# Batch 0's attention in halves of the heads, its loads on two queues, and a re-timed plan

## The chip, the cores and the metric

The kernel runs on one core of one Trainium2 chip. A time is the device time of one execution in microseconds. The core's engines run side by side: PE (matrix products; its weight loads are listed as PEld), DVE and ACT (elementwise work), POOL (here only constants and the issue of DMAs) and SP (only the issue of DMAs). Each works through its instructions in the order in which the program holds them, and waits for the others through semaphores. All DMAs, whoever issues them, run on the core's 16 DMA engines.

## The reference

Eight batches of a linear attention with eight heads of 64, 576 tokens each, and behind it a feed-forward block over all 4608 tokens:

```python
theta = np.pi / 2.0 * pos / S
def phi(x, c, s):
    r = np.maximum(x, 0.0)
    return np.concatenate([r * c, r * s], axis=-1)
q_p, k_p = phi(q, cos_w, sin_w), phi(k, cos_w, sin_w)
kv = np.einsum('bhsf,bhsd->bhfd', k_p, v)
z = np.sum(k_p, axis=2)
num = np.einsum('bhsf,bhfd->bhsd', q_p, kv)
den = np.einsum('bhsf,bhf->bhs', q_p, z)[..., None] + 1e-06
x = (num / den).transpose(0, 2, 1, 3).reshape(B * S, H * D)   # 4608 x 512
h = x @ w_in                                                  # 512 x 2048
return (np.maximum(h, 0.0) ** 2) @ w_out                      # 2048 x 512
```

## The kernel before

A batch has 576 tokens: 512 "main" ones, held as 128 partitions of J = 4 columns (a token's place is 4p + j), and a tail of 64. The tail of heads 0 to 3 lies on partitions 0 to 63, that of heads 4 to 7 on 64 to 127; `HH` = 4 is half the heads.

Attention of a batch: load k, q (tile `kq`), v and their tails (`kqt`, `vst`); form the features (`cos_part`, `sin_part`: a relu times a column of cosines or sines, into `fe`; `cos_tail`, `sin_tail` into `fet`); copy v into `vext`, which has a column of ones for the sums z; sum k'v over the tokens on PE (`mm_kv`, into `kz`) and copy it out (`kvz`); transpose the query features (`tq`, copied to `qpT`); form numerators and denominators in one product (`mm_num`, into `num`); divide (`div`: add EPS into `den`, reciprocal, multiply into `xp`); and transpose x (`tx`, copied to `xT`). Batches 0 and 1 transpose on PE, later ones by DMA from SP's queue.

The feed-forward block: h = x w1 in units of 128 tokens x 2 by 256 columns (`hps`), then relu (`rt`) and square (`gT`), then the second product. Batch 0 and the first 16 units each of batches 1 and 2 are plain sums (`plan_plain1`); the others, and the second products of all batches but the first (`plan_pair`), use a seven-product scheme for 2 x 2 blocks, with sums of inputs made on DVE (`xs`, `w1s`, `w2t`, `gs`) and outputs combined from PSUM.

The opening, `begin`, is an order written out by hand. SP loads all of k. POOL issues the k tails, v, v's tails, then the constants (an iota; ACT makes the cosine and sine columns of it), the queries of columns 0 and 1 and of columns 2 and 3, four quarters of w1, the q tails, the first quarter of w2, and behind that batch 1's loads. PE multiplies zeros meanwhile (`warm`, 31 times, and some more further on). Then batch 0's first 256 tokens (columns 0 and 1) go through the whole attention, all eight heads at once: features of k, sums, features of q, transposes, numerators, division, x transposes. `xT` for these 256 tokens is complete when both columns' copies are done; the first units of the feed-forward block work on 128 tokens at a time, so that they can begin behind the first copy.

Everything behind the opening is ordered by a planner. Each step (`plan.op`) has its engine or engines, a modelled duration and what it follows; `plan.timeline` and `plan.dues` give due times back from the order of PE's products; `plan.run` goes through modelled time and lets each engine take the ready step with the smallest due time plus `SHIFT`. Steps that may run on ACT or DVE go where they would end first, unless `PINS` fixes them. What the opening leaves is told to the planner by `plan.given` with a time (when a w1 quarter has landed, when xT is there), and `plan.run` starts each engine at a given time. The planner's times decide the order of the instructions alone: on the chip an instruction runs when its inputs are there. The planner gives the product `mm_num` 0.49 us for a main column.

Of the kernel before, what the change touches and what calls it, by code (L numbers as in the profile page):

```python
# [24 lines left out]
    "qT0.3": -31.9, "xT0.4": 32, "H0.0.10.128": 13.4, "H0.0.11.0": 43.7, "H0.2.11.0": 11.5,  # L25
    "H0.3.11.0": 54.4, "cos1.2": -59.2, "sin1.2": -74.7, "cos1.3": -14, "qT1.0": 0.9,
    "num1.2": 43.7, "num1.3": 39.3, "xTc1.3": 132.4, "num1.4": 28.6, "Y0.5": -38.6, "Y0.6": -125,
    "w2t2": -56.9, "vs2.2": -129.7, "cos2.t": -52.5, "num2.4": 10.7, "H1.0.00.0": 55.6,
    "H1.0.01r": -26.6, "H1.1.00.0": 61.4, "H1.1.10.0": 30.6, "H1.1.01r": 32.5, "H1.2.10.0": 20.8,
    "H1.2.10q": -36.8, "H1.2.01q": -5.3, "H1.2.11.0": 68.3, "H1.3.00.0": 7.6, "ldv3.0": 13.8,  # L30
    "cos3.1": -16.4, "sin3.1": -8, "qTd3.1": -71.6, "qTd3.2": 11.2, "num3.4": 9,
    "H2.0.11.0": 10.4, "H2.2.10.0": 9.9, "H2.2.01.0": -74.6, "H2.3.00.0": 3.2, "H2.3.10.0": 44,
    "H2.3.10r": 24, "H2.3.11.0": -11.9, "Y1.P2": 25.1, "Y1.P5": -11.2, "Y1.P4": -63.2,
    "ldk4": -67.5, "cos4.0": 14.7, "cos4.2": 27.1, "sin4.3": 51.1, "xTd4.2": 62, "xs3.1": -57.3,
    "xs3.2": -36.1, "xs3.3": -21.9, "G3.1.P5": 7.9, "G3.1.P3": -74.8, "G3.1.c12q": -2.5,
    "G3.1.P4": 166.2, "G3.1.c21r": 6.2, "G3.2.P1": -10.4, "G3.2.P2": 13.6, "G3.2.c11r": 10.9,
    "G3.2.c12r": 3, "G3.2.c22q": 83.4, "G3.3.P5": 11.5, "G3.3.P2": 48, "Y2.P1": 45.5,
    "Y2.P6": 9.2, "Y2.P7": -8.1, "ldv5.0": -8.1, "sin5.1": -8.4, "cos5.2": -23.5, "sin5.2": -0.6,
    "sin5.3": -20.9, "num5.2": -9.7, "num5.3": -80.6, "G4.0.c21r": 93.6, "G4.1.c11q": 71,
    "G4.1.c12r": 1.5, "G4.1.c21q": 9.9, "G4.2.seed": -97.7, "G4.2.c11q": 9.2, "G4.2.P6": -0.3,  # L40
    "G4.2.P3": 7.6, "G4.2.c12r": 85.9, "G4.2.P4": 5.7, "G4.3.P5": 13.4, "G4.3.P6": 78.6,
    "Y3.S3": 42.1, "Y3.P6": -2.9, "Y3.P2": -11.9, "Y3.c12": 40.2, "ldq6": 30.5, "vs6.1": 87.7,
    "sin6.1": 32.5, "cos6.2": -22.7, "sin6.3": 55, "num6.0": 18.7, "div6.1": -32, "xTd6.0": 30.9,
    "num6.4": 28.3, "G5.0.c22r": 24.3, "G5.1.P3": 29.5, "G5.1.P7": -12, "G5.2.P7": 62.7,
    "G5.3.P7": -22.1, "G5.3.c22q": 8.8, "Y4.P2": -35.3, "Y4.P7": 59.5, "Y4.P5": 52.2,
    "Y4.c12": -21.2, "ldk7": -71.6, "ldkt7.1": -12.6, "num7.2": 38.6, "G6.0.P1": 17,
    "G6.0.P3": 44.1, "G6.0.P7": 30.6, "G6.2.P3": 69.8, "G6.2.c22q": 2, "G6.3.P1": -21.1,
    "G6.3.c12r": 53.8, "G6.3.c22r": -2, "Y5.P5": 68.2, "Y5.P3": 91.4, "G7.0.P4": 8.3,
    "G7.1.P7": 29.7, "G7.2.P7": 5.6, "G7.2.P4": 13.6, "G7.3.c12q": 16.8, "G7.3.c21q": 19.7,
    "Y6.P3": 22.2, "xs8.3": -26.6, "G8.1.P1": -33.6, "G8.2.P3": 16.2, "Y7.P7": 45.6,  # L50
    "Y7.P4": 15.3, "Y8.P20": 42.1, "Y8.P21": 43.7,
# [8 lines left out]
        "H0.1.01r H0.2.11q cos1.1 cos1.2 sin1.2 cos1.3 qTc1.1 xTc1.3 vs2.2 sin2.0 sin2.1 "  # L60
        "H1.3.01q cos4.0 cos4.1 cos4.2 sin4.3 sin4.t G3.2.c11q G3.2.c22q G3.2.c21q cos5.0 "
        "sin5.t G4.1.c12q G4.2.c11q G4.3.c11q G4.3.u2 G4.3.c22q Y3.s5 vs6.1 sin6.1 sin6.t "
        "G5.0.c21q G5.2.c11q G5.2.c22q vs7.0 vs7.2 G6.3.c22q"
    ),
    "DVE": (
        "H0.2.11r vs2.0 sin2.t H1.1.00r H1.2.01q H1.3.00r G3.1.c12q G3.1.c21r vs5.1 sin5.1 "
        "sin5.2 G4.0.c11q G4.1.c11q G4.1.c21q G4.2.c12q Y3.c21 vs6.2 G5.0.s5 G5.0.c22q "
        "G5.1.c11r G5.1.c21r G5.1.c21q G5.3.c22q G6.0.c11r G6.2.c22q G7.3.c12q G7.3.c21q "
        "G8.0.c11r Y8.s5"
# [290 lines left out]
def kernel(  # L360
# [215 lines left out]
    def load_main(nm, b, eng, j0=0, j1=J):  # L576
        eng.dma_start(
            out=kq[b][:, "kq".index(nm)][:, :, j0:j1], in_=main_of(nm, b)[:, :, j0:j1]
        )
# [22 lines left out]
    def fe_main(b, j, c0, c1, a=slice(0, 2)):  # L602
        return fe[b, j // 2][:, a, j % 2, :, c0:c1]

    def kq_main(b, j, a=slice(0, 2)):
        return kq[b][:, a, :, j, :]

    def cos_part(e, b, j, a=slice(0, 2)):
        feature(e, fe_main(b, j, 0, D, a), kq_main(b, j, a), cos_col[:, j : j + 1])

    def sin_part(e, b, j, a=slice(0, 2)):
        feature(e, fe_main(b, j, D, F, a), kq_main(b, j, a), sin_col[:, j : j + 1])

    def cos_tail(e, b, a=slice(0, 2)):
        feature(e, fet[b][:, a, :, 0:D], kqt[b][:, a], cos_col[:, J : J + 1])

    def sin_tail(e, b, a=slice(0, 2)):
        feature(e, fet[b][:, a, :, D:F], kqt[b][:, a], sin_col[:, J : J + 1])

    def mm_kv(b):  # L620
        for j in range(J + 1):
            for hh in range(HH):
                for half in range(2):
# [949 lines left out]
```

## Time and profile before

Three runs: 279.78, 281.14 and 284.09 us, median 281.14. The profiled execution took 279.59, of which its instructions span 277.4.

| what | from the profiled execution |
|---|---|
| busy share of the span | PE 97%, PE weight loads 82%, DVE 84%, ACT 66%, POOL 10% |
| granted PE clock | 0.999 on average |
| DMA | 53.00 MB, mean 191 GB/s |
| k of batch 0, 1 MB on SP, from issue to landing | 5.6 us |
| v of batch 0, 1 MB on POOL, from issue to landing | 7.6 us |
| last product on PE | starts 270.21, 1.91 us for the group of 16 |
| mean duration on DVE | 128x512 feature of batch 0 547 ns, its 128x256 tail 473, 128x1024 feature 760, square 420, relu from PSUM 688, `xp` 692, `vext` 128x1024 691 |
| mean duration on ACT | 128x512 feature 713 ns, 128x256 493, square 629, relu from PSUM 592, `qpT` 128x512 585 |

"PE" in the profile's lists is a product, "tile<-inputs" what it writes and reads; a group is several instructions of one kind in a row, and its length runs to the modelled end of the last, so that the next group can start before it.

### The profile page before, as it was taken

The numbers are of one execution on the slowest core, as the hardware profiler recorded it, in microseconds if no ns is written. First come the engines' busy times: TensorE is split into PE (matmuls) and PEld (weight loads), VectorE is DVE, ScalarE is ACT, GpSimd is POOL, SyncE is SP. The second block draws the span as 40 slices with busy tenths as digits, with TensorE's granted clock in tenths as the row PEclk, the third lists the DMA queues.
The fourth block names the chain that finished last, engine by engine and source line by source line (L and its number), as shares of the span: only waits on it lengthen the run. The fifth ranks groups of instructions, "written<-read, shape, count | busy, mean of one in ns | idle before, by whom it ended". The sixth has DMA issues, their size and how long they took to land.

```text
span 277.4 us, 6927 instructions
## 1 busy us (share of the span) xinstructions
PE 268.6 (97%) x2835; PEld 226.5 (82%) x2835; DVE 231.7 (84%) x453; ACT 184.3 (66%) x309; POOL 28.4 (10%) x46
## 2 busy tenths in 40 slices
PE   8999999999999999999999999999999999999992
PEld 2579856789889889888898888898888888888881
DVE  1779877898996979999999999999889959977921
ACT  3758863596967697699478967974457556756210
POOL 8835454100000000000000000000000000000000
PEclk9999999999999999999999999999999999999999
DMA  6999999989899999988876999751140001201014
GB/s 222 319 206 288 312 267 337 354 216 358 158 244 338 229 246 220 370 166 264 269 248 119 289 241 269 206 152 40 46 174 14 2 0 76 78 0 78 0 78 151
DMA packets 77503, 53.00 MB, mean 191 GB/s; under 512 B 52097, under 2 KB 72577, under 8 KB 77473
## 3 DMA queue, kind: packets, MB, share of 16 engines
q1 hardware_dynamic: 70128, 38.28, 51.6%
q0 software_dynamic: 7024, 13.76, 18.7%
q10 hardware_dynamic: 320, 0.52, 0.6%
q8 instruction: 22, 0.36, 0.6%
q14 instruction: 9, 0.07, 0.1%
HBM read 36.70 MB, written 9.44 MB: 166 GB/s over the span
## 4 chain that ended last, share of the span: by engine, by line
PE 74%; DMA 18%; DVE 3%; ACT 2%; issue 1%; POOL 0%; POOLq 0%; ACTq 0%; DVEq 0%
PE ya L537 17%; PE yb L537 15%; PE hb L537 11%; DMA kq<-in_q_dram 9%; PE hc L537 7%; PE ha L537 7%; PE hps L537 7%; DMA xT<-xp 4%; PE wm L537 4%; DMA vs<-in_v_dram 3%; PE kz L537 3%; PE num L537 2%; DMA qpTt<-fet 2%; PE yc L537 1%; ACT fe L524 1%
## 5 line engine op out<-in xcount | busy, mean ns | idle before, releaser
L537 PEld LDWEIGHTS <-w1sb 128*128 128x128 bf16 x800 | 73.8, 98 | 11.0 <-issue 2.7
L537 PEld LDWEIGHTS <-gs 128*128 128x128 bf16 x512 | 49.9, 98 | 6.0 <-DVE gs L534 0.2
L518 ACT ACTIVATE gT<-rt 128x512 bf16<-128x512 bf16 x77 | 47.5, 629 | 10.4 <-DVE rt L531 5.1
L537 PEld LDWEIGHTS <-gT 128*128 128x128 bf16 x448 | 43.5, 98 | 10.8
L537 PE MATMUL hps<-xT,w1sb 128*128 128x256 bf16 (+1 forms) x416 | 46.1, 264 | 1.1 <-ACT rt L512 0.4
L524 ACT ACTIVATE fe<-kq,cols 128x1024 bf16<-128x1024 f32 (+1 forms) x35 | 35.2, 1046 | 3.5 <-DMA kq<-in_q_dram 2.8
L537 PE MATMUL ya<-w2sb,gT 128*128 128x256 bf16 x256 | 30.6, 273 | 0.0
L537 PEld LDWEIGHTS <-w1s 128*128 128x128 bf16 x288 | 27.4, 98 | 3.6 <-issue 0.5
L520 DVE TENSOR_TENSOR gT<-rt 128x512 bf16<-128x512 bf16 x67 | 27.2, 420 | 3.7 <-ACT rt L512 3.0
L526 DVE TENSOR_SCALAR fe<-kq,cols 128x1024 bf16<-128x1024 f32 (+1 forms) x37 | 24.9, 714 | 5.5 <-DMA kq<-in_k_dram 5.1
L537 PE MATMUL hb<-xs,w1sb 128*128 128x256 bf16 x192 | 28.0, 273 | 0.0
L512 ACT ACTIVATE rt<-hps 128x512 bf16<-128x512 f32 x33 | 19.3, 592 | 7.5 <-PE hps L537 7.3
L537 PE MATMUL ha<-xT,w1sb 128*128 128x256 bf16 x160 | 24.0, 273 | 0.1
L663 DVE TENSOR_TENSOR xp<-num,den 128x512 bf16<-128x512 f32 (+1 forms) x33 | 22.3, 675 | 1.1
L534 DVE TENSOR_TENSOR gs<-gT 128x2048 bf16<-128x2048 bf16 x16 | 19.5, 1220 | 0.1
L531 DVE CUSTOM_DVE_ANT_0 rt<-hb,s 128x512 bf16<-128x512 f32 x24 | 16.3, 686 | 1.0 <-PE hb L537 0.7
L531 DVE CUSTOM_DVE_ANT_0 rt<-hc,u 128x512 bf16<-128x512 f32 x24 | 16.4, 685 | 0.2 <-PE hc L537 0.2
L508 ACT COPY hb<-ha 128x512 f32<-128x512 f32 x24 | 14.0, 581 | 4.0 <-DVE y L534 2.3
L508 ACT COPY u<-hb 128x512 f32<-128x512 f32 x22 | 12.8, 584 | 4.9 <-PE hb L537 4.9
L537 PE MATMUL yb<-w2sb,gs 128*128 128x256 bf16 x128 | 15.3, 273 | 0.0
L537 PE MATMUL yb<-w2t,gs 128*128 128x256 bf16 x128 | 15.3, 273 | 0.0
L537 PE MATMUL yb<-w2t,gT 128*128 128x256 bf16 x128 | 15.3, 273 | 0.0
(112 smaller groups left out, 401.1 us busy)
## 6 DMA issues: line engine op xcount, KB each, us to landing
out_dram<-y SPq DMA_DIRECT2D x16, 512.0 KB, 4.4
kq<-in_k_dram SPq DMA_DIRECT2D x6, 1024.0 KB, 6.2
kq<-in_q_dram SPq DMA_DIRECT2D x5, 1024.0 KB, 7.9
vs<-in_v_dram SPq DMA_DIRECT2D x10, 512.0 KB, 5.0
w1sb<-in_moe_w_in_dram POOLq DMA_DIRECT2D x4, 512.0 KB, 10.6
w2sb<-in_moe_w_out_dram POOLq DMA_DIRECT2D x4, 512.0 KB, 11.0
kq<-in_q_dram POOLq DMA_DIRECT2D x2, 1024.0 KB, 12.0
kq<-in_k_dram POOLq DMA_DIRECT2D x2, 1024.0 KB, 11.1
```

What stands on the lines that cost most here:

```text
L508: (nc.scalar.copy if e == "ACT" else nc.vector.tensor_copy)(out=out, in_=in_)
L512: nc.scalar.activation(out=out, in_=in_, func=ACTF.Relu)
L518: nc.scalar.activation(out=out, in_=in_, func=ACTF.Square)
L520: nc.vector.tensor_tensor(out=out, in0=in_, in1=in_, op=ALU.mult)
L524: nc.scalar.activation(out=out, in_=in_, func=ACTF.Relu, scale=col)
L526: nc.vector.tensor_scalar(out=out, in0=in_, scalar1=0.0, scalar2=col, op0=ALU.max, op1=ALU.mult)
L531: nc.vector._custom_dve(dve_ops.TENSOR_ADD_SAT, out=out, in0=in0, in1=in1, s0=BIG, s1=0.0)
L534: nc.vector.tensor_tensor(out=out, in0=in0, in1=in1, op=op)
L537: nc.tensor.matmul(out=out, lhsT=lhsT, rhs=rhs, start=start, stop=stop, skip_group_check=True)
L663: nc.vector.tensor_tensor(out=x.rearrange("p (b k) (l d) -> p b k l d", b=n, l=2), in0=n4[:, :, :, 0:D].rearrange("p b (k l) d -> p b k l ...
```

## The change

Three things.

Batch 0's opening works on two groups of four heads (A: heads 0 to 3, B: heads 4 to 7), one behind the other, with both columns of a group together. SP loads, for each group, k, the k tail and the v tail; POOL loads v and the queries of columns 0 and 1 for each group, with the constants between, then the first w1 quarter, the queries of columns 2 and 3, and the other w1 quarters. The order of the steps is written out anew, with 17 warming products at the start and others between the steps. The copies of `xT` go by kb (two of the four rows of x each), and the first two units of the feed-forward block are emitted in two parts each: kb 0 and 1, which need group A alone, and kb 2 and 3. All units now work on 256 tokens at a time; before, the first column's units of batch 0 worked on 128.

The planner's duration of a main numerator goes from 0.49 to 0.26, and the given times of the opening from 15.9 to 14.6 (first w1 quarter), 17.2 to 17.4 (features of columns 2 and 3), 13.3 to 12.6 (`kvz`), 16.4 and 17.4 to 14.2 and 15.6 (`xT`); the engines start at 14.6, 17.2 and 16.8 in place of 16.8, 17.4 and 17.1 (PE, ACT, DVE).

The tables `SHIFT` and `PINS` are replaced by others. The set of batches in plain sums (`PLAIN`) is the same in both.

```diff
 PINS = {
     "ACT": (
-        "H0.1.01r H0.2.11q cos1.1 cos1.2 sin1.2 cos1.3 qTc1.1 xTc1.3 vs2.2 sin2.0 sin2.1 "
...
+        "H0.0.01r sin2.t cos3.t H2.2.00q G3.2.s5 G3.3.c21q G4.0.c22q vs6.2"
...
             f"num{b}.{j}",
-            {"PE": 0.49 if j < J else 0.25},
+            {"PE": 0.26 if j < J else 0.25},
...
+        for part in range(parts):
+            kbs = range(part * KB // parts, (part + 1) * KB // parts)
...
         for g in range(2):
-            load_tail("k", 0, g, nc.gpsimd)
-        nc.gpsimd.dma_start(out=v0[:, :, :, :], in_=main_of("v", 0))
+            load_main("k", 0, nc.sync, heads[g])
+            load_tail("k", 0, g, nc.sync)
+            nc.sync.dma_start(out=vt0[rows_[g]], in_=tail_of("v", 0, g))
         for g in range(2):
-            nc.gpsimd.dma_start(out=vt0[g * TAIL : (g + 1) * TAIL], in_=tail_of("v", 0, g))
-        constants()
-        for i in range(2):
-            load_main("q", 0, nc.gpsimd, 2 * i, 2 * i + 2)
-        warm(31, "x0")
...
+            nc.gpsimd.dma_start(out=v0[:, heads[g]], in_=main_of("v", 0)[:, heads[g]])
+            load_main("q", 0, nc.gpsimd, heads[g], first)
+            if g == 0:
+                constants()
         for i in range(4):
             load_w1(i, 4)
+            if i == 0:
+                load_main("q", 0, nc.gpsimd, js=second)
...
+        def key_features(g, sin_tail_on):
+            for j in range(J):
+                cos_part("DVE", 0, j, k_, heads[g])
+                sin_part("ACT", 0, j, k_, heads[g])
+            cos_tail("DVE", 0, k_, rows_[g])
+            sin_tail(sin_tail_on, 0, k_, rows_[g])
+
+        def values(g):
+            dst = vx[:, :, heads[g], 0:D].rearrange("p j h d -> p h j d")
+            copy("DVE", dst, v0[:, heads[g]])
+            copy("DVE", vxt[rows_[g], :, 0:D], vt0[rows_[g]])
...
+        warm(17, "x0")
+        key_features(0, "ACT")
+        values(0)
+        za = kv_sums(0, "x1")
+        query_features(0)
+        kv_copy(0, za)
+        warm(1, "x0")
+        ta = turn_queries(0, "x2")
+        copy_queries("DVE", 0, ta, 0)
+        copy_queries("ACT", 0, ta, 1)
+        warm(3, "x0")
+        na = spare("n0", [P, 2, FP], F32, "num")
+        numerators(0, na)
+        key_features(1, "DVE")
+        div_den(na[:, :], dens[0])
+        values(1)
+        warm(6, "x0")
+        zb = kv_sums(1, "x3")
+        query_features(1)
+        div_mul(na[:, :], dens[0], x_of(0))
+        kv_copy(1, zb)
+        tb = turn_queries(1, "x4")
+        copy_queries("DVE", 1, tb, 0)
+        copy_queries("ACT", 1, tb, 1)
+        warm(3, "x0")
+        nb = spare("n0", [P, 2, FP], F32, "num")
+        numerators(1, nb)
+        xa = turn_x(0, "x5")
+        div_den(nb[:, :], dens[1])
+        div_mul(nb[:, :], dens[1], x_of(1))
+        for kb in range(2):
+            copy_x("ACT", 0, xa, kb)
+        warm(5, "x0")
+        xb = turn_x(1, "x1")
+        copy_x("DVE", 1, xb, 0)
+        copy_x("ACT", 1, xb, 1)
+        for j in (2, 3):
+            cos_part("DVE", 0, j, q_)
+            sin_part("ACT", 0, j, q_)
...
-        plan.timeline(rows, 16.8)
+        plan.timeline(rows, 14.5)
         plan.dues()
-        order = plan.run({"PE": 16.8, "ACT": 17.4, "DVE": 17.1, "POOL": 36.0, "SP": 46.0}, 44.2)
+        order = plan.run({"PE": 14.6, "ACT": 17.2, "DVE": 16.8, "POOL": 36.0, "SP": 46.0}, 44.2)
```

`numerators` writes a group's numerators of both columns into one tile, so that `div_den` and `div_mul` each treat the group's two columns in one instruction; `turn_queries`, `turn_x` and their copies do the transposes of one group.

## The prediction

> **What bounds the kernel now.** I read the page's busy times first, then the stages, then who PE waits for, then the opening in order of time, then the DMA issues. On the page:
>
> ```profile
> span 277.4 us, 6927 instructions
> ...
> PE 268.6 (97%) x2835; PEld 226.5 (82%) x2835; DVE 231.7 (84%) x453; ACT 184.3 (66%) x309; POOL 28.4 (10%) x46
> ```
>
> PE is the bound. The stages (stretch, its length, busy time by engine, granted clock, DMA share, GB/s) say where it is not:
>
> ```profile
> 0.00:4.00 4.00, 2.81 (x7) 1.01 (x8) 0.38 (x4) 1.28 (x1) 2.94 (x8) 1.00 0.41 116
> 4.00:8.00 4.00, 4.00 (x13) 1.43 (x12) 1.57 (x3) 1.99 (x5) 3.72 (x10) 1.00 1.05 375
> 12.00:17.00 5.00, 4.57 (x55) 2.78 (x56) 4.57 (x15) 4.12 (x7) 1.33 (x2) 1.00 1.24 215
> 22.00:272.00 250.00, 248.33 (x2647) 214.33 (x2645) 218.62 (x418) 172.07 (x289) 13.54 (x19) 1.00 0.69 186
> ```
>
> From 22 us to the last product PE idles 1.67 us in 250. The clock is 1.00 in every row. So the end moves only with the moment at which PE's real work begins, or with those 1.67 us. PE's waits after 18 us, largest first, are three of 0.3 to 0.4 us, of three kinds:
>
> ```profile
> PE hps L537 <- ACT rt L512: 0.4, 1, 0.4
> PE hc L537 <- DVE xs L534: 0.3, 1, 0.3
> PE hps L537 <- DMA xT<-xp: 0.3, 1, 0.3
> ```
>
> The opening in order of time (start, length, idle before in brackets): PE's 9.77 us of warming products are no work, and the first real product (hps) starts at 17.09.
>
> ```profile
> 1.19 9.77 PE L537 MATMUL wm<-zeros 128*128 128x512 bf16 x31 [1.19 <-DVE zeros L441]
> ...
> 11.81 1.33 ACT L524 ACTIVATE fe<-kq,cols 128x512 bf16<-128x512 f32 x2 [0.94 <-DMA kq<-in_q_dram]
> ...
> 17.09 0.61 PE L537 MATMUL hps<-xT,w1sb 128*128 128x128 bf16 x8
> ...
> 18.37 1.06 PE L675 MATMUL tq<-ident,fe 128*128 128x128 bf16 x16
> 19.27 1.06 PE L537 MATMUL hps<-xT,w1sb 128*128 128x128 bf16 x16
> 20.16 0.41 PE L537 MATMUL num<-kvz,qpT 128*128 128x65 bf16 x8
> ```
>
> DMA issues (KB, us from issue to landing), for issues of 7.9 to 10.4 us and then of 37 to 40 us:
>
> ```profile
> w1sb<-in_moe_w_in_dram POOLq DMA_DIRECT2D x3, 512.0 KB, 10.0
> ```
> ```profile
> kqt<-in_k_dram SPq DMA_DIRECT2D x2, 64.0 KB, 8.0
> kqt<-in_q_dram SPq DMA_DIRECT2D x2, 64.0 KB, 12.0
> ```
>
> The second quarter of w1 (issued at 8.81) thus lands at about 18.8; and 64 KB on SP takes 8 to 12 us while POOL's queue streams.
>
> **The opening, part by part.** Before, batch 0 needs k, v, both tails and the first two query columns, 2.75 MB, and the last of it releases the features at 11.81. From there it takes 6.1 us to the second copy of xT, which ends at 17.88 (17.29 + 0.59).
>
> After, the same 2.75 MB stand ahead of everything else, so I take group B's queries (heads 4 to 7) to land at the same 11.8 at the latest. The first 4 us move at 116 GB/s where the next 4 run at 375, because SP's k load has the engines to itself; POOL now issues v at 1.26 instead of 2.63. That can be worth between 0 and 0.9 us; I take 0.3: 11.5.
>
> From group B's queries to xT, everything is half as wide: sin on ACT twice (0.49 and 0.40, from the 128x256 row's 493 ns less the overlap of the 128x512 pairs) 0.9; hop and last transposes 0.5; ACT copy of qpT 128x512 0.59; hop, numerators, hop 0.5; den and reciprocal 0.17 + 0.20 + 0.07 of gaps; xp 128x512 0.69; x transposes with hops 0.5; copy 128x256 0.42 (the ACT row of xTt). The sum is 4.5: xT is complete at 16.0, against 17.88.
>
> This holds if DVE, which is in order, keeps up. Between group A's qpT copy and group B's xp it has, at its rows (128x256 features 0.27 to 0.41, bounded by the 128x256 cast and the 128x256 features of the tail; 128x1024 cast 0.69; 128x512 xp 0.69; half kvz 0.34 to 0.42; qpT 0.41; den pairs 0.37): eight features, two casts, two kvz/qpT copies, two xp and two den pairs, 5.5 to 6.7 us. Group A must then be through its qpT copy by 9.5 or so. A's inputs are 1.4 MB; before, 1.39 MB had moved by 6.4 us. So A's queries land between 6.4 (the two queues share evenly) and 9.3 (POOL's first transfer waits until SP's six loads are through, as it seems to before: the k tails that POOL issued at 1.26 took 5.0 us, landing just behind SP's k). I take 7.5; A's features, transposes and copy add 1.9: 9.4. That is just in time, and each us later moves xT by one.
>
> What comes next on PE is not xT alone. The built order is: two units (each in two parts by kb), 16 query transposes, one unit of the next column block, a numerator, then the rest. That third unit needs w1's second quarter. Its place in the byte order is unchanged (batch 0's loads, the first w1 quarter and the last query columns are all ahead of it, in either order), so it lands at 18.8, or up to 0.9 sooner. With xT at 16.0 the two units end at 17.0, the features of columns 2 and 3 (ACT, 1.33 behind the xT copy) at 17.3, the transposes at 18.2, and the third unit starts at 18.85, held by w1. Before, the same unit comes after the numerator's 0.25, at 20.41; without that, 20.16. The gain is 1.3 us. It stays 1.3 for any xT up to 16.5; from there on it shrinks one to one (third unit = xT + 2.3) and is nothing at 17.9. The parts are costed at nothing: w1's landing covers them; without that cover the first parts of both units, which can run before xT is complete, are worth up to 0.9.
>
> The 128-wide units become 256-wide: sixteen pairs take 0.89 (19.27 to 20.16), eight of the others 0.87 (a group of 16 at 0.109 each); four units give 0.1. Warming products fall from 39 to 35; they run only where PE waits anyway: nothing, and up to 0.9 if four of them (0.22 each) stood late in the chain. DVE's fet and vextt halves on 64 partitions add four instructions of 0.27 to 0.41, counted above.
>
> **The plan.** Of a numerator, the next product starts 0.25 behind it (20.16 to 20.41): the plan's 0.49 was 0.24 too much for some 30 of them, 7 us of plan time in which PE was really ahead. No instruction goes away. New shifts and pins move work between engines: in the built program DVE has 18 fewer relus and 13 more squares, six more wide features; at 0.69, 0.42 and 0.76 us that leaves DVE some 2 to 5 us lighter. Neither engine was the bound. Batch 2's first product, which waited 0.3 us for xT by DMA, now has three of batch 1's output products (1.75 us each) before it in place of two, so it does not need that transfer sooner. Loads for batches 1 and 2 keep their order on POOL except that k's second tail now stands behind the k and q loads; their DMA time is unchanged and PE has Y0's 14 us as cover. The idle 1.67 us can go to 0 or double; I take it as it is.
>
> **Sum.** 279.59 (profiled run: span 277.4 and 2.2 around it) less 1.3 gives 278.3. The three runs before are 279.78, 281.14, 284.09; the profiled one lies 1.5 under their median. I put the median after half a us above the sum: 278.8.
>
> **Rivals.**
>
> 1. *SP's second half starves.* SP's third to sixth loads (64 KB, 512 KB, 64, 64) run beside POOL's stream, and the rows above give 8 and 12 us to 64 KB there. Group B's v tail is issued at about 3.7 (0.46 and 0.65 each on SP), so it lands between 11.7 and 15.7. It decides from about 12.5 on, when DVE reaches that cast; DVE is in order, so everything behind waits. At 15.3, xT is complete at 20.0, the third unit starts at 22.3 instead of 20.16, and the kernel takes 281.7, slower than before. For it: the two rows. Against it: those SP tails were issued into a POOL queue already full, these at the very start. [...]
> 2. *POOL starts behind SP.* A's v lands at 8.6 and its queries at 9.3, DVE's chain ends at 18.2, third unit at 20.5: 279.9, no change. For it: the 5.0 us above.
> 3. *More.* The queues share from 3 us on and w1 lands 0.9 sooner, with 1.0 of the 1.67 us gone: 276.4.
> 4. *The tighter plan opens waits in the body*: 7 batches at one further wait of 0.4 (the largest now): 278.3 + 2.8 = 281.1.
> 5. *PE's clock falls in the longer waits of the opening.* The 31 warming products show the two rates: the weight loads come every 0.43 us up to 7.13, then 16 in 3.34. Seventeen end at about 7.8, and then PE waits for each group. If it fell back, some 6 us at half rate (1.19 to 7.13) cost 3: 281.3. [...]
>
> **Numbers.** Chances: forecast 0.47, rival 1 0.15, rival 2 0.13, rival 3 0.14, rival 4 0.07, rival 5 0.04. Range: 276.2 (rival 3) to 282.4 (rival 1, half a us over its sum); it leaves out combinations. 2% is 5.6 us, about what a measurement can tell from no change. Faster by that needs more than the opening's 1.3 to 2.2, all idle time and a lucky median: 0.06, from rival 3. Slower by that needs rivals 1 and 4 or 5 together: 0.07. Within: 0.87.
>
> **What would show it.** In the changed profile: the first hps at 14.5 to 15.5; the third unit's wait ended by the w1sb DMA, near 18.8; the first numerator behind it 1.3 us earlier than now; PE idle after 22 us near 1.7. Rival 1 shows as DVE's vextt or fet waiting for an SP load past 12.5, rival 2 as vext released past 8.5. The prediction is wrong if PE waits somewhere in the body for more than 1 us.

## The result, and the profile after

| | before | after |
|---|---|---|
| median of four runs each, us | 280.94 (279.78 to 284.09) | 283.15 (282.95 to 284.49) |
| ratio after to before | | 1.0103 (95% interval 1.0053 to 1.0152) |
| profiled execution, us (span) | 279.59 (277.4) | 282.95 (280.4) |
| xT of the first 256 tokens complete, us | 17.88 | 20.86 |
| third unit starts, us | 20.16 without the numerator before it | 23.11 |
| last product ends, us | 272.12 | 274.99 |

The ratio is one of means, without the run before at 284.09, which fell into a slower state. The changed kernel is 1.0% slower, outside the forecast range and on the other side of no change. The page of the changed kernel, its span and busy times:

```profile
span 280.4 us, 6877 instructions
...
PE 266.6 (95%) x2799; PEld 225.6 (80%) x2799; DVE 228.2 (81%) x454; ACT 186.2 (66%) x321; POOL 27.2 (10%) x44
```

PE is busy 2.0 us less than before (268.6), and the span is 3.0 us longer: PE waits about five us more. The stages of the changed kernel say where (stretch, its length, busy us and instruction count of PE, PE weight loads, DVE, ACT and POOL, granted clock, DMA share, GB/s):

```profile
0.00:4.00 4.00, 2.81 (x7) 1.03 (x8) 0.38 (x4) 1.68 (x3) 2.66 (x11) 1.00 0.45 142
4.00:8.00 4.00, 3.32 (x11) 1.20 (x10) 1.31 (x4) 1.71 (x4) 4.00 (x7) 1.00 0.91 242
8.00:12.00 4.00, 2.32 (x36) 1.61 (x35) 2.91 (x8) 1.47 (x4) 2.59 (x3) 1.00 1.10 354
12.00:17.00 5.00, 3.52 (x44) 2.17 (x43) 4.23 (x14) 2.83 (x7) 1.43 (x2) 1.00 1.19 256
17.00:23.00 6.00, 5.19 (x54) 3.52 (x53) 3.65 (x10) 3.42 (x7) 0.62 (x1) 1.00 1.24 210
23.00:275.00 252.00, 249.39 (x2657) 216.11 (x2654) 215.27 (x416) 175.13 (x298) 15.94 (x23) 1.00 0.69 184
```

Behind 23 us PE idles 2.6 us in 252, where it idled 1.67 in 250 before. It is also busy 0.8 us less from the third unit to the last product (249.28 for 250.04), so that this way is as long as it was (251.71 us before from the unit behind the numerator, 251.88 after). Its two longest waits (us in total, times, longest) are new:

```profile
PE ha L516 <- ACT hb L487: 1.1, 1, 1.1
PE yb L516 <- DVE y L513: 0.8, 1, 0.8
```

The first, at 105.6 us, is a wait of over 1 us in the body, which the prediction had named as a sign of being wrong. On balance it cost nothing, since the way is no longer. The whole loss lies ahead of the third unit. There the DMA engines move 242 GB/s between 4 and 8 us, where before they moved 375. PE in the opening, in order of time (start, length, what, idle before in brackets):

```profile
9.68 0.67 PE L516 MATMUL kz<-vext,fe 128*128 128x65 bf16 x16 [2.36 <-DVE vext L487]
...
15.22 0.67 PE L516 MATMUL kz<-vext,fe 128*128 128x65 bf16 x16 [1.15 <-DVE vext L487]
...
18.20 0.30 PE L516 MATMUL num<-kvz,qpT 128*128 128x65 bf16 x4 [0.32 <-ACT qpT L487]
...
19.96 0.60 PE L516 MATMUL hps<-xT,w1sb 128*128 128x256 bf16 x4
20.91 1.47 PE L516 MATMUL hps<-xT,w1sb 128*128 128x256 bf16 x12 [0.35 <-ACT xT L487]
...
23.11 1.04 PE L516 MATMUL hps<-xT,w1sb 128*128 128x256 bf16 x8
```

The first real product starts at 19.96 (17.09 before), and the third unit 2.25 us behind a complete xT, as the forecast had it. PE waits for DVE's casts of v, twice. The list of DVE in the same stretch carries the rest:

```profile
8.68 0.34 DVE L505 TENSOR_SCALAR fet<-kqt,cols 64x256 bf16<-64x256 f32 x1 [2.75 <-DMA kqt<-in_k_dram]
8.95 0.68 DVE L487 CAST vext<-v 128x1024 bf16<-128x1024 f32 x1
9.55 0.49 DVE L487 CAST vextt<-vt 64x256 bf16<-64x256 f32 x1
9.96 0.74 DVE L505 TENSOR_SCALAR fe<-kq,cols 128x256 bf16<-128x256 f32 x2
10.63 0.41 DVE L487 CAST kvz<-kz 128x260 bf16<-128x260 f32 x1
11.38 0.42 DVE L487 COPY qpT<-tq 128x512 bf16<-128x512 bf16 x1 [0.34 <-PE tq L1431]
11.88 1.14 DVE L505 TENSOR_SCALAR fe<-kq,cols 128x256 bf16<-128x256 f32 x4
13.55 0.62 DVE L505 TENSOR_SCALAR fet<-kqt,cols 64x256 bf16<-64x256 f32 x2 [0.53 <-DMA kqt<-in_k_dram]
...
14.53 0.64 DVE L487 CAST vext<-v 128x1024 bf16<-128x1024 f32 x1
15.31 0.29 DVE L487 CAST vextt<-vt 64x256 bf16<-64x256 f32 x1
...
18.54 0.17 DVE L642 TENSOR_SCALAR den<-num 128x8 f32<-128x8 f32 x1 [1.01 <-PE num L516]
```

DVE has done A's key features by 5.93, waits 2.75 us for A's k tail, and goes through two passes from there: 11.8 us lie between A's last input (the v tail, landed at 9.02) and xT, of which DVE is idle 2.8. It reaches B's vextt at 15.17 and has to wait only 0.14 for the load that landed at 15.29. The chain of waits goes to that very load:

```profile
4.00 11.29 DMA vt<-in_v_dram
15.29 0.02 issue
15.31 0.29 DVE vextt L487
```

That is how a page can mislead: the load ended last by a tenth of a microsecond, and whether it is the cause can't be read from it. The same holds for these DMA rows (KB, median us from issue to landing), the small ones of which took as long as the large ones:

```profile
v<-in_v_dram POOLq DMA_DIRECT2D x2, 512.0 KB, 7.3
...
vt<-in_v_dram SPq DMA_DIRECT2D x2, 64.0 KB, 9.1
```

B's three loads on SP, one by one:

```profile
kq<-in_k_dram SPq DMA_DIRECT2D x1, 512.0 KB, 9.1
...
kqt<-in_k_dram SPq DMA_DIRECT2D x1, 64.0 KB, 10.2
vt<-in_v_dram SPq DMA_DIRECT2D x1, 64.0 KB, 11.3
```

B's keys (the first row) were issued at 2.71 and so landed at about 11.8, just when DVE came to them (its qpT copy ended at 11.80). No wait shows, and yet, by the order of DVE's list, an A group that was on time would have left DVE waiting there.

### The profile page after: what moved, and what is told of

It reads as the page before. It is cut to its first block, busy times and chain, and to the rows that moved or that the text cites. A ratio compares the mean times of both kernels' runs of the same rounds, so it can differ in the third digit from the quotient of the medians.

```text
span 280.4 us, 6877 instructions
## 1 busy us (share of the span) xinstructions
PE 266.6 (95%) x2799; PEld 225.6 (80%) x2799; DVE 228.2 (81%) x454; ACT 186.2 (66%) x321; POOL 27.2 (10%) x44
## 4 chain that ended last, share of the span: by engine, by line
PE 77%; DMA 11%; DVE 7%; issue 2%; SPq 1%; ACT 1%; DVEq 0%; ACTq 0%
PE ya L516 16%; PE yb L516 13%; PE hb L516 11%; PE hps L516 8%; PE ha L516 7%; PE hc L516 7%; PE yh L516 5%; DMA vt<-in_v_dram 4%; DMA xT<-xp 4%; DMA kq<-in_q_dram 4%; PE num L516 3%; DVE fe L505 3%; PE kz L516 3%; PE tq L667 1%; PE yc L516 1%
## 5 line engine op out<-in xcount | busy, mean ns | idle before, releaser
L516 PEld LDWEIGHTS <-w1sb 128*128 128x128 bf16 x768 | 73.0, 98 | 11.0 <-issue 1.8
L516 PE MATMUL hps<-xT,w1sb 128*128 128x256 bf16 x384 | 45.7, 273 | 0.5 <-ACT xT L487 0.3
L497 ACT ACTIVATE gT<-rt 128x512 bf16<-128x512 bf16 x64 | 39.8, 630 | 8.4 <-DVE rt L510 6.9
L499 DVE TENSOR_TENSOR gT<-rt 128x512 bf16<-128x512 bf16 x80 | 32.2, 419 | 3.8 <-ACT rt L491 3.2
L505 DVE TENSOR_SCALAR fe<-kq,cols 128x1024 bf16<-128x1024 f32 (+2 forms) x49 | 29.2, 645 | 3.9 <-DMA kq<-in_k_dram 3.3
L503 ACT ACTIVATE fe<-kq,cols 128x1024 bf16<-128x1024 f32 (+2 forms) x35 | 30.1, 901 | 1.3 <-DMA kq<-in_k_dram 0.7
L491 ACT ACTIVATE rt<-hps 128x512 bf16<-128x512 f32 x41 | 23.8, 594 | 6.1 <-PE hps L516 5.9
L648 DVE TENSOR_TENSOR xp<-num,den 128x512 bf16<-128x512 f32 x32 | 22.1, 691 | 1.1
L510 DVE CUSTOM_DVE_ANT_0 rt<-hb,s 128x512 bf16<-128x512 f32 x24 | 16.4, 685 | 2.6 <-PE hb L516 2.4
L510 DVE CUSTOM_DVE_ANT_0 rt<-hc,u 128x512 bf16<-128x512 f32 x24 | 16.4, 684 | 2.5 <-PE hc L516 2.5
L491 ACT ACTIVATE rt<-ha 128x512 bf16<-128x512 f32 x21 | 12.5, 596 | 6.6 <-PE ha L516 6.5
L516 PE MATMUL yb<-w2t,gT 128*128 128x256 bf16 x128 | 15.3, 272 | 0.8 <-DVE y L513 0.8
L516 PE MATMUL yb<-w2t,gs 128*128 128x256 bf16 x128 | 15.3, 273 | 0.1
L516 PE MATMUL yh<-w2sb,gT 128*128 128x512 bf16 x64 | 15.3, 379 | 0.0
```

What stands on the lines that cost most here:

```text
L491: nc.scalar.activation(out=out, in_=in_, func=ACTF.Relu)
L497: nc.scalar.activation(out=out, in_=in_, func=ACTF.Square)
L499: nc.vector.tensor_tensor(out=out, in0=in_, in1=in_, op=ALU.mult)
L503: nc.scalar.activation(out=out, in_=in_, func=ACTF.Relu, scale=col)
L505: nc.vector.tensor_scalar(out=out, in0=in_, scalar1=0.0, scalar2=col, op0=ALU.max, op1=ALU.mult)
L510: nc.vector._custom_dve(dve_ops.TENSOR_ADD_SAT, out=out, in0=in0, in1=in1, s0=BIG, s1=0.0)
```

## The experiments

Theories at the start. **S**: B's small loads on SP starve beside POOL's stream and are the cost by themselves (rival 1). **D**: group A is late, and behind it stand two passes through the in-order DVE. **P**: the new tables and numerator times open waits in the body (rival 4). All twelve runs, with the landing of the last input that each group needs, from the traces:

| run | median us | ratio to before (95%) | A's last input | B's last input | xT complete | third unit |
|---|---|---|---|---|---|---|
| before | | 1 | 11.78, no groups | | 17.88 | 20.41 |
| after | 283.15 | 1.0103 (1.0053 to 1.0152) | 9.02 | 15.29 | 20.86 | 23.11 |
| 1 B's tails on POOL | 283.94 | 1.0080 (1.0052 to 1.0108) | 8.56 | 12.62 | 20.10 | 22.36 |
| 2 all tails on POOL | 282.78 | 1.0056 (1.0024 to 1.0088) | 9.36 | 12.30 | 20.85 | 23.10 |
| 3 = 2, B's keys first | 282.88 | 1.0031 (0.9990 to 1.0071) | 9.39 | 11.99 | 20.33 | 22.58 |
| 4 before, new plan | 281.17 | 0.9987 (0.9959 to 1.0015) | 11.43, no groups | | 17.54 | 20.07 |
| 5 new loads alone | 285.71 | 1.0165 (1.0129 to 1.0201) | 15.38, no groups | | 23.43 | 25.95 |
| 6 halves alone | 284.53 | 1.0098 (1.0049 to 1.0148) | 12.71 | 12.71 | 23.38 | 25.63 |
| 7 = 3, more warming | 281.96 | 1.0024 (0.9995 to 1.0053) | 9.57 | 12.44 | 20.08 | 22.33 |
| 8 = 7, reordered | 280.94 | 0.9984 (0.9957 to 1.0012) | 8.73 | 11.80 | 18.53 | 20.78 |
| 9 after, own tiles | 282.89 | 1.0066 (1.0030 to 1.0102) | 9.22 | 15.59 | 20.34 | 22.40 |
| 10 = 8, own tiles | 281.20 | 0.9985 (0.9950 to 1.0019) | 8.61 | 11.74 | 17.70 | 19.77 |
| 11 order with new loads | 282.86 | 1.0059 (1.0028 to 1.0090) | 8.81 | 14.96 | 20.29 | 22.54 |
| 12 = 10, old plan | 301.27 | 1.0715 (1.0670 to 1.0760) | 8.59 | 11.47 | 17.32 | 20.62 |

In before and in runs 4, 5 and 12 a numerator of 0.25 us stands ahead of the third unit, in the others behind it. The times of xT separate what the ratios, with intervals of 0.3 to 0.5%, often don't. But each xT is read in one execution, and landings vary: with the same loads A's last input came between 8.59 and 9.57 (runs 2, 3, 7, 8, 10, 12). A few tenths of a us in xT are not an edit's alone.

**1. B's two tails on POOL**, between B's v and B's queries; the other loads as changed.

```diff
...
         for g in range(2):
             nc.gpsimd.dma_start(out=v0[:, heads[g]], in_=main_of("v", 0)[:, heads[g]])
+            if g == 1:
+                load_tail("k", 0, g, nc.gpsimd)
+                nc.gpsimd.dma_start(out=vt0[rows_[g]], in_=tail_of("v", 0, g))
             load_main("q", 0, nc.gpsimd, heads[g], first)
```

> The changed kernel with one difference: group B's two 64 KB tails (k and v) are issued by POOL, between B's v and B's queries, not by SP. Theory S (B's small SP loads, which landed at 13.53 and 15.29 in the changed kernel, hold the opening by themselves, as the chain of waits says): they land near 12.3, xT is complete near 18 in place of 20.86, and the profiled execution is some 2.5 to 3 us shorter than the changed kernel's. Theory D (group A's data came late, its last at 9.02, and DVE's work in order behind it sets xT; DVE waited only 0.53 and 0.14 us for B's tails): xT moves by 0.7 at most, to about 20.2, and so does the time.

B's tails land at 12.03 and 12.21 in place of 13.53 and 15.29, and xT comes 0.76 us sooner. But A's last input came 0.46 us sooner too, and from that input to xT it is still 11.54 us (11.84 in the changed kernel). That is near D's forecast (0.7 at most) and far from S's (xT near 18).

**2. All tails on POOL**, each behind its v; SP loads the two halves of k alone.

```diff
         for g in range(2):
             load_main("k", 0, nc.sync, heads[g])
-            load_tail("k", 0, g, nc.sync)
-            nc.sync.dma_start(out=vt0[rows_[g]], in_=tail_of("v", 0, g))
         for g in range(2):
             nc.gpsimd.dma_start(out=v0[:, heads[g]], in_=main_of("v", 0)[:, heads[g]])
+            load_tail("k", 0, g, nc.gpsimd)
+            nc.gpsimd.dma_start(out=vt0[rows_[g]], in_=tail_of("v", 0, g))
             load_main("q", 0, nc.gpsimd, heads[g], first)
```

> The changed kernel with SP issuing only the two halves of k; POOL issues the tails of each group behind that group's v and ahead of its queries. Theory D: group A's last input lands near 8.0 and its k tail near 7.3 in place of 8.66, so DVE's chain starts over 1.5 us sooner and has no wait left at B's tails: xT complete near 17.2, the third unit near 19.4 (in place of 23.11), 3 to 4 us less than the changed kernel, a little below the kernel before. Theory S: the same as with B's tails alone on POOL.

D's forecast (A's last input near 8.0, xT near 17.2) missed: A's inputs came no sooner (9.36). B's tails landed at 11.57 and 11.77, and xT is complete at 20.85, as in the changed kernel. DVE of this run:

```profile
11.77 1.47 DVE L505 TENSOR_SCALAR fe<-kq,cols 128x256 bf16<-128x256 f32 x4
13.27 0.71 DVE L505 TENSOR_SCALAR fet<-kqt,cols 64x256 bf16<-64x256 f32 x2
...
15.00 0.29 DVE L487 CAST vextt<-vt 64x256 bf16<-64x256 f32 x1
15.32 0.93 DVE L505 TENSOR_SCALAR fe<-kq,cols 128x256 bf16<-128x256 f32 x2
```

No bracket: the tails lay there for 1.7 and 3.2 us before DVE came to them. S as the cause by itself falls. That xT did not move at all has a part of chance: the 0.67 us that DVE had waited for B's tails in the changed kernel are gone, but A's last input came 0.34 later and the features took 0.7 longer (last section).

**3. B's main key features ahead of A's tail**, on top of run 2 (k of B lands at 5.8 there, and DVE was idle until 8.7).

```diff
-        def key_features(g, sin_tail_on):
+        def key_main(g):
...
+        key_main(0)
+        key_main(1)
         key_features(0, "ACT")
```

> As the kernel with all tails on POOL, and with DVE and ACT forming group B's eight main key features right behind group A's, ahead of A's values, where DVE idled for 2.75 us in the changed kernel. Theory D: 1.1 to 1.8 us of DVE work leave the chain, xT complete near 15.8, the third unit then held by w1's second quarter near 19: 0.3 to 0.6 us less than with the tails alone. Theory S: no difference from that kernel.

xT at 20.33, far from D's 15.8: 0.52 us for 1.47 us of DVE work (run 2's row at 11.77) taken out of the list. A clock that fell is new in it. Stages of this run, same columns as above:

```profile
8.00:10.00 2.00, 0.26 (x9) 0.26 (x9) 1.26 (x4) 1.51 (x5) 1.33 (x2) 1.00 1.03 342
10.00:12.00 2.00, 2.00 (x28) 1.49 (x25) 1.31 (x4) 0.32 (x1) 2.00 (x3) 0.76 0.58 115
12.00:14.00 2.00, 2.00 (x14) 0.89 (x12) 1.55 (x6) 1.39 (x3) 2.00 (x4) 0.50 1.16 189
14.00:16.00 2.00, 2.00 (x27) 1.26 (x26) 1.94 (x5) 0.00 (x0) 1.88 (x3) 0.89 1.10 328
```

PE idled 3.23 us (6.51 to 9.74); from 11.0 to 14.4 it was granted half the clock, and three warming products took 0.43 us each in place of 0.22, and the eight numerators 0.64 in place of 0.43 (run 8).

**4. The kernel before with the changed plan**: the new shifts and pins and the 0.26 for a numerator; loads, steps and given times of before.

```diff
...
-            {"PE": 0.49 if j < J else 0.25},
+            {"PE": 0.26 if j < J else 0.25},
```

> The kernel before with the changed kernel's shifts and pins and its 0.26 us for a numerator, the opening untouched. If the plan has no part in the loss (theories S and D, by the body: from the third unit to the last product 251.9 us in the changed kernel, 252.0 before), the time is within 0.7 us of the kernel before. If the plan costs (theory P), it is 1 to 3 us slower.

0.9987, with 1 in the interval: the plan costs nothing that can be measured, and P falls as the cause of the 1% (the upper end of the interval is 0.4 us). The profiled execution idles 3.89 us in the body, though, against 1.67, with a wait of 1.31 at 75.6 for a transfer of x. The wait of 0.8 for y stands in every run with the new plan, and neither in before nor in run 5.

**5. The new loads alone**, in the kernel before, which computes all heads at once.

```diff
-        load_main("k", 0, nc.sync)
...
+        for g in range(2):
+            load_main("k", 0, nc.sync, heads[g])
+            load_tail("k", 0, g, nc.sync)
+            nc.sync.dma_start(out=vt0[rows_[g]], in_=tail_of("v", 0, g))
+        for g in range(2):
+            nc.gpsimd.dma_start(out=v0[:, heads[g]], in_=main_of("v", 0)[:, heads[g]])
+            load_main("q", 0, nc.gpsimd, heads[g], first)
...
```

> The kernel before with the changed kernel's loads alone (SP: k, k tail, v tail for each half of the heads; POOL: v and the first queries for each half, constants between, w1's first quarter ahead of queries 2 and 3); the whole-head order of the steps and the old plan stay. Theory S (the small SP loads are the cost by themselves): vt of B lands near 15.3, its vext copy, which stands ahead of the query features on DVE, waits for it, xT is complete near 20.8, and the kernel takes 283 to 284. Theory D (the two passes of the in-order DVE are the cost, the loads only set when they begin): the whole-head order still needs all its inputs at once, so vt of B at 15.3 delays it too; S and D agree here to about 0.5 us, and the run gives the price of the loads without the halves: xT 20.5 to 21.2. If vt of B lands before 12, both miss and xT stays near 18.

The v tail of B landed at 15.38, as expected, but xT came at 23.43, 2.2 us beyond the upper end of the expectation. The expectation had left out B's keys, which landed at 11.9: this order forms the key features of all heads at once, and DVE began them at 12.06. PE had idled 4.44 us ahead of the sums and had half the clock from 12.1 to 18.95. The loads alone, with that clock, make the kernel 1.65% slower, against 1.03% with the halves.

**6. The halves alone**, with the loads of before.

```diff
...
+        load_main("k", 0, nc.sync)
+        for g in range(2):
+            load_tail("k", 0, g, nc.gpsimd)
+        nc.gpsimd.dma_start(out=v0[:, :, :, :], in_=main_of("v", 0))
+        for g in range(2):
+            nc.gpsimd.dma_start(out=vt0[rows_[g]], in_=tail_of("v", 0, g))
+        constants()
+        load_main("q", 0, nc.gpsimd, js=first)
...
```

> The changed kernel's order of steps in halves of the heads and its plan, with the loads of before (k whole on SP; on POOL the k tails, v whole, v tails, constants, first queries of all heads, queries 2 and 3, w1). All inputs are there by 11.8. Theory D: group A can begin its casts only at 10.2 and its query features at 11.8, and behind them stand two passes of DVE; from A's last input to xT the four runs with halves took 10.9 to 11.8 us, of which B's key features, 2.6, can't move ahead in this order: xT 21.5 to 23.4, the kernel 284 to 286. Theory S: without the small SP loads the halves are harmless: xT 17.9 or earlier, the kernel 281 or less.

xT at 23.38, as D has it: with all inputs there at 12.71, the order in halves takes 10.7 us to xT, and the order of before 6.1. Half the clock (9.6 to 16.4) is a part of it. Each of the two changes alone is no better than both together (xT at 23.43 and 23.38, against 20.86), though half the clock stood in these two runs and not in the changed kernel's profile. The order in halves, as built, is long with either set of loads, and the new loads are late with either order.

**7. More warming at the start**, on top of run 3: 28 products for 17, and none for six ahead of B's sums.

```diff
-        warm(17, "x0")
+        warm(28, "x0")
...
-        warm(6, "x0")
```

> The run with B's key features moved ahead (all k on SP, tails on POOL), with 28 warming products at the start in place of 17 and none ahead of B's sums in place of six. By the clock: the 3.23 us of PE idle ahead of A's sums go to about 0.9, the warming products behind them run at 0.22 us each in place of 0.43, the query transposes of A at 0.5 in place of 0.83, the numerators at 0.2 in place of 0.64; A's numerators come about 1.0 us sooner and xT is complete at 19.0 to 19.6 in place of 20.33; the kernel about 0.7 to 1.3 us less than that run. If the clock was no part of the chain, xT stays within 0.3 of 20.33.

PE's wait ahead of A's sums is 0.94 us, and the eight query transposes of A behind it take 0.61 us, as in the changed kernel with its clock at 1.00, in place of run 3's 0.83; xT is at 20.08. That is 0.25 us sooner, and the expectation for xT missed: the faster products ran into waits for DVE (1.35 us of PE ahead of B's sums), since A's division still stood ahead of B's casts. A's last input also came 0.18 us later, and the cast of B's v took 0.94 us for 0.64. The clock was a small part of the chain.

**8. DVE's order rewritten**, on top of run 7: B's casts (half of them on ACT) and query features ahead of A's division, B's kvz and qpT copies ahead of A's multiply; the sine of B's tail on ACT, and four warming products fewer further on.

```diff
...
+        value_half("ACT", 1, second)
         copy_queries("DVE", 0, ta, 0)
...
-        key_features(1, "DVE")
-        div_den(na[:, :], dens[0])
-        values(1)
+        key_features(1, "ACT")
+        value_half("DVE", 1, first)
+        copy("DVE", vxt[rows_[1], :, 0:D], vt0[rows_[1]])
         zb = kv_sums(1, "x3")
         query_features(1)
-        div_mul(na[:, :], dens[0], x_of(0))
+        div_den(na[:, :], dens[0])
         kv_copy(1, zb)
...
         copy_queries("ACT", 1, tb, 1)
+        div_mul(na[:, :], dens[0], x_of(0))
...
```

> The same, and DVE's order rewritten: half of B's main values and the sine of its tail go to ACT, B's casts and query features stand ahead of A's division, and A's division ahead of B's numerators; two warming products fewer in two places. Theory D: DVE's list between A's last input (9.0 to 9.4) and xT falls from some 9.3 us to 8.3 and B's sums no longer wait for A's numerators: xT complete at 17.3 to 18.2, the third unit at 19.6 to 20.5, near the kernel before (17.88 and 20.41) or up to 0.8 us ahead of it: 280.5 to 281.8. If what is left is the loads (theory S), xT stays above 19.

xT at 18.53, 1.55 us sooner and 0.3 later than D's range. The gain is the order's: A's inputs landed 0.84 sooner, but DVE copied A's queries at 11.62 as in run 7 (11.63), behind the 28 warming products. The kernel is level with before and, by the two ratios, 1.2% ahead of the changed one. DVE of this run:

```profile
12.97 0.29 DVE L487 CAST vextt<-vt 64x256 bf16<-64x256 f32 x1
13.29 0.80 DVE L505 TENSOR_SCALAR fe<-kq,cols 128x256 bf16<-128x256 f32 x2
...
16.21 0.17 DVE L642 TENSOR_SCALAR den<-num 128x8 f32<-128x8 f32 x1 [0.53 <-PE num L516]
```

B's v tail is cast at 12.97 and B's division begins at 16.21; in the changed kernel that was 15.31 and 18.54.

**9. Tiles of their own.** In the changed kernel, the query transposes of both columns share one PSUM tile, DVE copies one column out of it and ACT the other; likewise xT. ACT in the changed kernel:

```profile
17.55 0.59 ACT L487 COPY qpT<-tq 128x512 bf16<-128x512 bf16 x1 [2.73 <-DVE qpT L487]
...
20.48 0.37 ACT L487 COPY xT<-tx 128x256 bf16<-128x256 bf16 x1 [1.08 <-DVE xT L487]
```

DVE's copies ended at 17.52 and 20.45. Run 9 is the changed kernel with a tile for each column and each kb, as the kernel before has it.

```diff
-            t = spare(tag, [P, 2, HH, P], BF16, "tq")
+            ts = [spare(tg, [P, HH, P], BF16, "tq") for tg in tag]
...
```

> The changed kernel with one edit: the query transposes of the two columns, and the x transposes of the two kb, go to a PSUM tile of their own each, as in the kernel before; loads, order and plan as changed. In all runs with halves ACT's copy of qpT and of xT begins 30 ns after DVE's copy out of the same tile ends (17.55 behind 17.52, 20.48 behind 20.45 in the changed kernel). If the shared tile is what holds it, ACT's copies begin with DVE's: B's numerators end 0.3 to 0.4 us sooner, the last xT copy another 0.3, xT complete near 20.1 to 20.3 in place of 20.86, the kernel 0.5 to 0.8 us less than the changed one. If it is something else (ACT late by itself), nothing moves.

ACT in this run is released by PE, and its copies overlap DVE's (17.40 to 17.82 and 19.85 to 20.14):

```profile
17.12 0.59 ACT L487 COPY qpT<-tq 128x512 bf16<-128x512 bf16 x1 [1.96 <-PE tq L1431]
...
19.96 0.37 ACT L487 COPY xT<-tx 128x256 bf16<-128x256 bf16 x1 [0.86 <-PE tx L1453]
```

xT at 20.34 in place of 20.86, with A's last input 0.2 us later: the shared tile holds the copies one behind the other, and that is worth 0.5 to 0.7 us (half the clock from 11.45 to 14.9 is in this run's 20.34). What the traces show is a whole copy waiting for the other's signal: out of the shared tile ACT's began 0.03 us behind DVE's end, both times.

**10. Runs 8 and 9 together.** The edits are those shown.

> The reordered kernel with the same edit. There B's numerators wait for A's division (15.69), so only the last xT copy gains: xT complete at 18.1 to 18.3 in place of 18.53, the third unit near 20.4, the same as in the kernel before; the time within 0.3% of before.

xT at 17.70, 0.4 us sooner than expected (ACT's copy of A's queries, too, no longer waits), and the third unit at 19.77. That is 0.39 us ahead of the kernel before, if its numerator is left out there too (20.16). The time is not ahead: 0.9985, with 1 inside. In its profile PE idles 3.84 us in the body, 1.12 of them at 75.57 for a transfer of x, as in run 4; in run 8, whose third unit is one us later and whose order there is the same, nothing waits for that transfer.

**11. The new order with the changed kernel's loads**, run 8's warming products included; B's key features behind A's queries, B's sums behind B's query transposes.

```diff
-        key_features(1, "DVE")
+        key_main(1)
+        value_half("DVE", 1, slice(0, J))
+        query_features(1)
+        tb = turn_queries(1, "x4")
         div_den(na[:, :], dens[0])
...
+        key_features(1, "ACT")
...
+        copy("DVE", vxt[rows_[1], :, 0:D], vt0[rows_[1]])
+        zb = kv_sums(1, "x3")
```

> The reordered steps with the changed kernel's own loads: small tails on SP, B's key features behind A's queries since k of B lands at 11.9, B's sums moved behind B's query transposes. It tells what the order of DVE is worth with the loads as they are, and what the late tails cost once the order no longer hides them. vt of B lands near 15.3; from its cast: sums, kvz copy, numerators, division and x: xT complete at 19.3 to 20.0, between the reordered kernel's 18.53 and the changed kernel's 20.86. Theory D alone would give 18.5 to 18.9 (loads free), theory S alone 20.6 or later (order worth nothing).

xT at 20.29, later than expected: ACT's share of B's features held the transposes until 14.19, and PE's clock was at half from 15.8 to 19.2. Beside run 8 this is the main evidence: the order alone (11) gains 0.57 us, early tails and keys alone (2) 0.01, and both, with B's keys first, 2.33 (8). The two delays lie beside each other, and each hides what the other one costs. The two small gains are rough: half the clock is part of run 11's 20.29, later inputs and slower features are part of run 2's 20.85, and run 11 differs from 8 in more than the loads, since B's k comes late with them (DVE waited 0.27 us for it, until 11.79). But the 2.33 is four times their sum.

**12. Run 10 with the plan of before**: old shifts, pins, numerator times and given times.

```diff
-            {"PE": 0.26 if j < J else 0.25},
+            {"PE": 0.49 if j < J else 0.25},
...
-        plan.timeline(rows, 14.5)
+        plan.timeline(rows, 16.8)
```

> The reordered opening with tiles of its own (third unit at 19.77, 0.64 ahead of the kernel before's 20.41), with the planner's durations, given times, shifts and pins of the kernel before. The body idle of that run was 3.84 us against 1.67 before, in three pieces of 0.8 to 1.1 that the changed plan has in nearly all runs (near 75, 113 and 268 us). If the pieces come with the plan, the body idle is near 2 and the kernel 0.5 to 1 us ahead of before: ratio 0.996 to 0.999. If the shifts only fit the opening that they were made for, the idle is 3 or more and the ratio 0.999 to 1.005.

Neither: 7% slower, though the third unit starts at 20.62, behind a numerator as in the kernel before (20.41). PE idles 18.7 us in the body and is busy some 7 us longer there than in run 10, with half the clock three times for 3.4 us. Its waits in this run (us in total, times, longest):

```profile
PE num L537 <- DVE xp L669: 7.6, 8, 3.9
PE tx L693 <- ACT rt L512: 4.3, 1, 4.3
```

From 54 us on PE waits for work that stands late in the order. That the old shifts don't fit the steps of the new opening (whole units, the first in parts) is likely, but shifts, pins, durations and given times were put back together, and which of them did it was not tried. What a plan fitted to run 10's opening would give was not tried.

## Why the prediction was wrong, step by step

- **Group A's queries at 7.5**: A's queries landed at 8.94 and its last input, the v tail on SP, at 9.02; within the bounds (6.4 to 9.3), 1.5 late. The changed kernel moved 242 GB/s between 4 and 8 us, where the kernel before moved 375. The step asked for the queries alone; what released DVE was A's k tail on SP, at 8.66.
- **A's chain, 1.9: failed.** It took 2.79 (9.02 to 11.81). The step counted features, transposes and copy and left out what stands ahead of them in DVE's list: the casts of A's v, 0.68 and 0.49.
- **DVE from A's qpT copy to B's xp, 5.5 to 6.7: the step that failed most.** From 11.81 to the end of B's xp at 19.67 it took 7.86. The work itself came to 5.93 us, within the range; the terms as the prediction lists them add up to about 6.0 to 7.2. The waits were not in the sum: 0.53 and 0.14 for B's tails, and 1.01 for B's numerators, of which 0.43 is ACT's copy behind DVE's out of one tile.
- **From xp to xT, 0.92**: 1.19, the 0.3 more being again ACT's copy behind DVE's.
- Together: "just in time, and each us later moves xT by one" fits the sum, but only from A's side. A's copy 2.4 us late (9.4 to 11.81), a pass 2.2 longer (7.86 for the 5.7 that led to a complete xT at 16.0) and 0.3 at the end are the 4.9 between the forecast 16.0 and the measured 20.86. A's 2.4 were not A's alone: B's keys landed at 11.8, so that with these loads DVE could not have begun B's pass before, however early A had been.
- **w1's second quarter as the next bound, third unit at 18.85**: it landed at 19.29 and bound nothing. xT + 2.3 held (2.25).
- **B's queries at 11.5 and 4.5 us from there**: 12.67, and they were not the last; k's tail came at 13.53 and v's at 15.29. The sum took it that the loads on SP would be there by then.
- **The plan at no cost**: right for the time (run 4), but "does not need that transfer sooner" was wrong: where the opening is as early as before or earlier, batch 2's first product waited 1.31 (run 4) and 1.12 us (run 10) for x by DMA in the profiled executions. The forecast gain of 1.3 might have met that wait. How far the early opening is its cause stays open: in run 6, whose third unit starts at 25.63, PE waited 0.84 us for a transfer of x too, at 84.9.
- **Rival 1** named landings (v's tail at 15.3), place and sign, and came nearest with 281.7; but its price was not its own. DVE reached the cast of that tail at 15.17 and not at 12.5, and waited 0.14. With the tails early xT did not move (run 2); late loads cost only once DVE is not late itself (run 11 beside run 8). **Rival 2** (A's v at 8.6, queries at 9.3) was about right for A (7.92 and 8.94), and too low as it took DVE's chain from there as sized. **Rival 5** didn't happen in the profiled execution of the changed kernel (mean clock 0.997): its longest wait, 2.36, left the clock at 1.00. Two of the other three executions had 0.992 and 0.991, and no trace says where. It did happen in runs 3, 5, 6, 9 and 11. **Rival 3** did not happen. **Rival 4** did in a small way: 0.9 us more of waits in the body, with one of 1.06, but the body was no longer for it.

## What to carry to other kernels

Splitting a serial stage in two makes an in-order engine go through it twice (DVE here took 7.86 us from the copy of A's queries to the end of B's xp, where 5.5 to 6.7 were booked): write its whole list from the first group's last input to the stage's result, casts and waits for other engines included, before a gain is booked. Where two delays run beside each other, undoing one shows little (runs 2 and 11); undo both before either is cleared. A load that lands just as the engine comes to it (B's keys at about 11.8, DVE at 11.80) shows no wait, and still bounds what an earlier start is worth. Tables and times that steer a planner belong to the steps that they were fitted to: the same opening took 281.2 us with one set and 301.3 with another.

## What the hardware showed that was not expected

Half the clock was granted for 3.4 us in runs 3 (11.0 to 14.4), 9 (11.45 to 14.9) and 11 (15.8 to 19.2) and three times in run 12 (from 59.3, 100.3 and 209.5), and for 6.8, twice that, in runs 5 (12.1 to 18.95) and 6 (9.6 to 16.4). The waits of PE ahead of it were 3.23 us (run 3), 3.50 (9) and 4.44 (5 and 6); in run 11 it was 1.70, with PE busy for 0.63 of the 2.75 us from 11.25 to 14.0, while 2.36 in the changed kernel left the clock at 1.00. In run 3 the fall came 1.3 us after PE had begun to work again, in runs 5 and 6 it came 2.1 us into the wait. What decides whether and when a wait brings the clock down no run here shows. The row of the profile's page that shows the clock in 40 slices hides most of it, a slice being 7 us: the changed kernel has 9 in all but the last, and run 5 begins with 9, 8, 6, 9.

A feature of 128x256 on DVE took 0.33 to 0.35 us mostly, and up to 0.67 in run 2 and 0.73 in run 8. In the changed kernel the two longest of its opening, 0.53 (begun at 5.1) and 0.48 (at 10.2), ran while POOL was issuing DMAs; but so did two at 12.4 and 12.7, with 0.35 each, and two from 15.6 on took 0.35 with POOL idle. What lengthened them was not tested. In run 2 it came to 0.7 us: 1.47, 0.71 and 0.93 for three groups of features that took 1.14, 0.62 and 0.62 in the changed kernel, and this is in its 20.85.
